# Decay attention with a softplus FFN: product banks as separate tiles, weight pairs of one layer, a read-back of converted weights, and other queues for loads and stores

## The chip, the cores and the metric

The kernel runs on one core of one Trainium2 chip. The metric is the device time of one execution in microseconds (us), the median of several runs. TensorE (PE) does the matmuls, VectorE (DVE) and ScalarE (ACT) the elementwise work, GpSimd (POOL) a few sums; SyncE (SP) issues most DMA transfers from its queue, in the order of the program.

## What is computed

The reference has two stages. First a decay attention over 4 batches, 8 heads, 768 positions of 64 numbers, in blocks of 64 positions with a state carried from block to block:

```python
for b in range(nb):
    intra = einsum('bhic,bhjc->bhij', qb, kb) * Dmask        # lam ** (i - j), i >= j
    intra = einsum('bhij,bhjd->bhid', intra, vb)
    inter = einsum('bhid,bhde->bhie', qb * lam_pow, kv_state)
    out[:, :, sl] = intra + inter
    kv_state = lam_block * kv_state + einsum('bhsd,bhse->bhde', kb * rev_pow, vb)
```

Its output, as 3072 tokens of 512 numbers, goes through an FFN of width 2048:

```python
h = x @ w_in
g = maximum(h, 0) + log1p(exp(-abs(h)))      # softplus
out = g @ w_out
```

All is float32; the weights arrive as float64.

## The kernel before

**Matmuls.** Each FFN operand is split in two rounded parts, high and low, and each product is made of three matmuls (high by high, low by high, high by low), 128x128 weights by 512 columns. Such a matmul takes TensorE 0.227 us.

**Tiling.** The work runs in six chunks of 128 positions by 4 batches, 512 tokens each. A chunk has four attention units, one for each pair of heads (24 units g in all). A unit's inputs come as one tile `att` by two loads of 512 KB (`load_upto`, L86). For each unit: decayed keys (`k_decay`, L287, ACT) and queries (`q_decay`, L294, DVE), scores and state matmuls (`mm_scores`, L309 and L311), the mask (L336, DVE), the state's update (L341, DVE), the output (`mm_out`, L324 and L328), which is then copied out of PSUM (L373, L384 or L391).

**Chunks 0 and 1.** After a prologue written out as a table of steps, a loop runs the steps s = 4 to 31 (`for s in range(LAG, last)`): 16 blocks of 128 of the hidden width, for chunk 0 and then for chunk 1. A step has the first-layer matmuls of block s (`mlp1`, L419, 12 matmuls into a bank `h`), softplus and the split of the block before (`chain_act` L400 and `chain_hi` L404 on ACT, `chain_lo` L408 on DVE), and the second-layer matmuls of the block four steps before (`mlp2`, L436). In chunk 0 every third step holds a unit's scores and two steps later its output; in chunk 1 every second step is an `event`, which has the output of the last unit and the scores of the next.

**Conversion of weights.** In chunk 0 the float64 words are turned into high and low parts, two blocks (a pair) in each step: `w_scale` (L215) and `w_round` (L219) on ACT, `w_shift` (L223), `w_sign` (L227) and `w_add` (L233) on DVE in one step; `w_hi` (L236, ACT) and `w_lo` (L240, DVE) in the next one. `w_order` says which blocks make a pair. Before, a pair is one block of the second layer and one of the first, (f, 1) and (f + 4, 0). All converted weights stay in SBUF through chunk 1. During steps 8 to 23 `store_blocks` (L501 to L504) writes them to DRAM too, in g1 and g2 (first layer) and g3 (second layer). In chunk 1, for each two blocks, POOL forms sums of their quarters (`block_sums`), ACT and DVE split these (`store_sums`, L525 and L526, the tile `parts`), and SP stores them (L528, L529).

**Chunks 2 to 5.** These go in twos (2 with 3, 4 with 5) through a Strassen scheme with seven products where eight would be needed. Each of eight iterations i loads the weights of two blocks from DRAM (`load_w1` L535 and L536, `load_w2` L541) and forms, from weights and token sums prepared before, the products P1, P6, P5, P2, P7, P4, P3 (`product`, L577, six matmuls each). Additions on DVE join them; softplus and splits on ACT and DVE follow. The 24 second-layer matmuls (`rest`, L596) of the iteration before are set between the products. With chunks 2 and 3, each iteration also has an `event`. After the eight iterations, the second layer of the odd chunk runs as a stretch of pure matmuls. `finish` (L605, L607) copies a chunk's four output banks and stores them.

**PSUM.** There are four banks for outputs (`obank`), two single banks in turns (`bank`: `h`, `x`, `y`, `a`) and one tile of two banks (`work`). An iteration's P1 and P2 go to `a`, a single bank. P6, P7 and P4 go to `b_`, P5 and P3 to `c_`; before, both are halves of the one work tile `bc`. The additions that read them are `u2 = b_ + p1` (L737), `u3 = b_ + p1` (L744), `u3 += c_` (L745), `c21 = b_ + p1` (L750) and `u2 += c_` (L754).

**What sets the order.** The program is written in the order in which each engine runs it; nothing is reordered later. An engine waits where a tile that it reads is not written yet, or where a tile that it writes is still being read. For such a wait a tile is one thing, its halves are not told apart. Tiles come from pools of buffers: 21 of 8 KB a partition (`t8`: `att`, weights, outputs), 7 of 4 KB, 5 of 2 KB; a load into a buffer waits until the last reader of what was there is done, and holds up what stands behind it in its queue.

Of the kernel before, what the change touches and what calls it, by code (L numbers as in the profile page):

```python
# [32 lines left out]
def decay_attention_softplus_ffn(  # L33
# [79 lines left out]
    w_order = [(f, 0) for f in range(LAG)]  # L113
    for f in range(NF):
        w_order.append((f, 1))
        if f + LAG < NF:
            w_order.append((f + LAG, 0))
    NW = len(w_order)
# [123 lines left out]
    def w_of(f, which):  # L242
        j, i = divmod(w_order.index((f, which)), 2)
        return w_pairs[j][:, :, i]
# [165 lines left out]
    def mlp1(s, ps_=range(NP)):  # L410
# [4 lines left out]
        for p in ps_:  # L415
            cs = slice(p * 128, (p + 1) * 128)
            x = x_of(c, p)
            for n, (i, j) in enumerate(((0, 0), (1, 0), (0, 1))):
# [3 lines left out]
                )  # L422

    def mlp2(ss):
        c = ss[0] // NF
# [5 lines left out]
        for b in range(B):  # L431
            for s in ss:
                f = s % NF
                g, w = g_tiles[s], w_of(f, 1)
                for n, (i, j) in enumerate(((0, 0), (0, 1), (1, 0))):
                    nc.tensor.matmul(  # L436
                        o_tiles[c][b], lhsT=g[:, i, b * 128 : (b + 1) * 128], rhs=w[:, j],
                        start=f == 0 and n == 0, stop=f == NF - 1 and n == 2,
                    )
# [82 lines left out]
    def store_sums(i):  # L522
# [3 lines left out]
        nc.vector.tensor_sub(out=parts[:, 1], in0=sums, in1=parts[:, 0])  # L526
        parts = parts.bitcast(F32)
        nc.sync.dma_start(out=g1[i][:, :, 2:4], in_=parts[:, :, 0:2])  # L528
# [72 lines left out]
    def finish(c, b):  # L601
        if c not in obs:
            obs[c] = t8([128, B, 512], F32, f"ob{c}")
        copy = nc.vector.tensor_copy if b % 2 else nc.scalar.copy
        copy(out=obs[c][:, b], in_=outs[c, b])  # L605
        queue = nc.scalar if c == NCH - 1 and b % 2 == 0 else nc.sync
        queue.dma_start(out=out[b * S + c * C : b * S + (c + 1) * C, :], in_=obs[c][:, b])  # L607
# [37 lines left out]
    for s in range(LAG, last):  # L645
        if s + 1 in units_at:
            k_decay(units_at[s + 1])
            q_decay(units_at[s + 1])
        chain_act(s - 1)
        chain_hi(s - 1)  # L650
        chain_lo(s - 1)
        old, new = w_group(s - 1), w_group(s)
        if old:
            w_hi(*old)
        if new:
            w_scale(*new)
            w_round(*new)
        if old:
            w_lo(*old)
        if new:  # L660
# [19 lines left out]
        w_load(2 * s + (8 if s < 9 else 6))  # L680
        if s in units_at:
            load_upto(units_at[s] + 2)
        if s == NF - 2:
            load_upto(2 * NP + 2)
        if 8 <= s < 8 + NF:
# [13 lines left out]
        if s == last - 1:  # L699
            x_sums_early(2, 1)  # L700
    x_sums_late(2, 1)
    chain_act(last - 1)
    chain_hi(last - 1)
    chain_lo(last - 1)

    def old_seconds(ss, ends=False):
        return seconds(STD - 1, [(s % NF, g_tiles[s], w_of(s % NF, 1)) for s in ss], ends)

# [5 lines left out]
    for c in range(STD, NCH, 2):  # L714
        more = c + 2 < NCH
        lb = {}
        gs = {}
        for i in range(NF // 2):
            if i + 1 < NF // 2:
                load_w1(i + 1)  # L720
            load_w2(i)
            unit = nxt if more else None
            if unit is not None and unit < NG:
# [7 lines left out]
            p1, u2, u3, c21 = ta[:, 0], ta[:, 1], tb[:, 0], tb[:, 1]  # L731
            a, bc = bank(f"a{c}_{i}"), work(f"bc{c}_{i}")
            b_, c_ = bc[:, 0], bc[:, 1]
            product("P1", i, a)
            nc.scalar.copy(out=p1, in_=a)  # L735
            product("P6", i, b_)
            nc.vector.tensor_add(out=u2, in0=b_, in1=p1)  # L737
            product("P5", i, c_)
            product("P2", i, a, False)
# [17 lines left out]
            if unit is not None and unit <= NG:  # L757
                event(unit)
                load_upto(unit + 2)
                nxt += 1  # L760
# [71 lines left out]
```

## Time and profile before

| | |
|---|---|
| median of 3 runs | 649.57 us (649.55 to 650.25) |
| profiled execution, its own time | 651.41 us |
| its span in the profile | 649.6 us |
| mean granted TensorE clock | 0.991 |
| prologue and chunk 0 | 0 to about 137 us |
| chunk 1 | about 137 to 250 us |
| products of chunk 2 | 250 to 410 us |
| second layer of chunk 3 | 410.5 to 455.6 us |
| products of chunk 4 | about 456 to 593 us |
| second layer of chunk 5 | 592.6 to 645.7 us |

The profile is of one execution; times in it count from the span's start. Its rows name an instruction by engine, line and tiles (written <- read), with buffer numbers left out, and give its start and duration; x12 is a run of twelve alike; in brackets stands how long the engine was idle before and what ended that. A chain of waits follows the last instruction back to what released it. The waits add up who waited for whom. A windows row gives the stretch, its length, each engine's busy time and instructions, the granted TensorE clock (1.00 is full speed), the share of time in which DMA was busy, and GB/s.

### The profile page before, as it was taken

How to read it: one execution, taken by the hardware profiler on the slowest of the kernel's cores; microseconds unless marked ns; L12 is line 12 of the kernel's file. 1: busy time of each engine (PE TensorE's matmuls, PEld its weight loads, DVE VectorE, ACT ScalarE, POOL GpSimd, SP SyncE). 2: the span in 40 equal slices, each digit the busy share in tenths (PEclk: the TensorE clock that was granted, in tenths of full speed). 3: DMA queues.
4: the chain of work that ended last, by engine and by line, in shares of the span. 5: the costliest groups of instructions: out<-in, count | busy, mean ns of one | idle time of the engine just before them, and what ended most of it. 6: DMA issues, size and time to landing. Idle time of an engine off the chain costs nothing.

```text
span 649.6 us, 11970 instructions
## 1 busy us (share of the span) xinstructions
PE 595.5 (92%) x5203; PEld 469.9 (72%) x5203; DVE 307.4 (47%) x452; ACT 251.6 (39%) x408; POOL 51.2 (8%) x59
## 2 busy tenths in 40 slices
PE   8899999599889999798998988999888988889997
PEld 6677888477678877676776766888666777667886
DVE  7689998463456476424424333491232222223410
ACT  4678776441444354332233322550222222223310
POOL 2000000254333500000000000000000000000000
PEclk9999999899999999989999999999999999999999
DMA  8997455657885567597435440395089542300911
GB/s 302 407 406 264 163 186 188 227 179 237 294 268 192 180 216 287 180 399 289 172 132 182 174 164 31 112 423 210 0 346 420 189 153 98 122 1 16 362 75 66
DMA packets 37445, 135.01 MB, mean 208 GB/s; under 512 B 3600, under 2 KB 5648, under 8 KB 31248
## 3 DMA queue, kind: packets, MB, share of 16 engines
q1 hardware_dynamic: 37104, 133.71, 56.5%
q8 instruction: 41, 0.67, 0.4%
q10 hardware_dynamic: 288, 0.52, 0.2%
q14 instruction: 12, 0.10, 0.0%
HBM read 104.86 MB, written 29.36 MB: 207 GB/s over the span
## 4 chain that ended last, share of the span: by engine, by line
PE 63%; DVE 13%; DMA 13%; ACT 4%; SPq 3%; issue 3%; DVEq 0%; ACTq 0%
PE o L596 24%; PE bc L577 19%; DMA att<-in_att 9%; PE a L577 6%; PE o L436 5%; PE h L419 5%; DMA raw<-in_wts 3%; DVE tb L744 2%; DVE tb L745 2%; DVE tb L750 2%; DVE ta L737 2%; PE z L324 1%; DVE parts L526 1%; ACT parts L525 1%; SPq L86 1%
## 5 line engine op out<-in xcount | busy, mean ns | idle before, releaser
L596 PE MATMUL o<-w,g 128*128 128x512 f32 x816 | 192.7, 390 | 0.0
L596 PEld LDWEIGHTS o<-w,g 128*128 128x128 f32 x816 | 152.6, 188 | 32.0
L419 PE MATMUL h<-x,w 128*128 128x512 f32 x384 | 93.4, 394 | 0.0
L436 PE MATMUL o<-w,g 128*128 128x512 f32 x336 | 85.3, 403 | 7.4 <-ACT w L236 6.2
L577 PE MATMUL bc<-xcP,w1b 128*128 128x512 f32 x288 | 77.5, 404 | 14.9 <-DVE tb L750 12.5
L419 PEld LDWEIGHTS h<-x,w 128*128 128x128 f32 x384 | 71.0, 188 | 16.7 <-issue 1.2
L436 PEld LDWEIGHTS o<-w,g 128*128 128x128 f32 x336 | 63.9, 193 | 22.8 <-ACT w L236 7.0
L577 PEld LDWEIGHTS bc<-xcP,w1b 128*128 128x128 f32 x288 | 51.7, 188 | 38.3 <-DVE tb L750 19.4
L577 PE MATMUL bc<-xcP,w1a 128*128 128x512 f32 x192 | 51.3, 403 | 15.4 <-DVE ta L737 15.4
L577 PEld LDWEIGHTS bc<-xcP,w1a 128*128 128x128 f32 x192 | 34.9, 188 | 28.8 <-DVE ta L737 22.2
L577 PE MATMUL a<-xcP,w1a 128*128 128x512 f32 x192 | 50.0, 397 | 0.0
L744 DVE TENSOR_TENSOR tb<-bc,ta 128x512 f32<-128x512 f32 x16 | 11.1, 692 | 73.1 <-PE bc L577 73.1
L577 PEld LDWEIGHTS a<-xcP,w1a 128*128 128x128 f32 x192 | 36.9, 192 | 8.0
L287 ACT ACTIVATE kd<-att,rp 128x256 f32<-128x256 f32 x40 | 18.2, 504 | 61.2 <-DMA att<-in_att 61.2
L737 DVE TENSOR_TENSOR ta<-bc,ta 128x512 f32<-128x512 f32 x16 | 11.1, 692 | 60.0 <-PE bc L577 58.0
L741 ACT ACTIVATE la<-a 128x512 f32<-128x512 f32 x16 | 9.6, 599 | 74.2 <-PE a L577 74.2
L408 DVE TENSOR_TENSOR g<-l,g 128x512 fp32r<-128x512 f32 x32 | 23.2, 724 | 25.0 <-ACT g L404 24.8
L588 DVE TENSOR_TENSOR g<-lb,g 128x512 fp32r<-128x512 f32 x32 | 21.1, 690 | 22.1 <-ACT g L584 22.1
L294 DVE TENSOR_TENSOR qd<-att,lp 128x512 f32<-128x512 f32 x20 | 16.1, 805 | 32.5 <-DMA att<-in_att 32.5
L512 POOL TENSOR_TENSOR full<-w 128x512 f32<-128x512 f32 x16 | 21.4, 1360 | 117.9 <-PE o L436 114.7
L735 ACT COPY ta<-a 128x512 f32<-128x512 f32 x16 | 9.3, 584 | 53.6 <-PE a L577 53.6
L584 ACT CAST g<-lb 128x512 fp32r<-128x512 f32 x32 | 18.9, 620 | 20.3 <-PE o L596 20.3
(96 smaller groups left out, 701.9 us busy)
## 6 DMA issues: line engine op xcount, KB each, us to landing
w<-g SPq DMA_DIRECT2D x32, 1024.0 KB, 9.0
att<-in_att SPq DMA_DIRECT2D x48, 512.0 KB, 6.6
raw<-in_wts SPq DMA_DIRECT2D x32, 512.0 KB, 10.2
w1a<-g SPq DMA_DIRECT2D x16, 1024.0 KB, 8.3
g<-w SPq DMA_DIRECT2D x24, 512.0 KB, 7.4
w1b<-g SPq DMA_DIRECT2D x16, 768.0 KB, 8.9
g<-parts SPq DMA_DIRECT2D x16, 512.0 KB, 4.3
out_dram<-ob SPq DMA_DIRECT2D x22, 256.0 KB, 2.2
```

The lines of the kernel that those rows point to most:

```text
L287: nc.scalar.activation(kd[:, :, t], kt_of(g)[:, :, t], AF.Copy, scale=rp1[:, h : h + 1])
L294: eng.tensor_mul(out=qd[r].rearrange("q b t i -> q b (t i)"), in0=q_of(g)[r].rearrange("q b t i -> q b (t i)"), in1=w)
L408: nc.vector.tensor_sub(out=g[:, 1, :], in0=l_tiles.pop(s), in1=g[:, 0, :])
L419: nc.tensor.matmul(h_tiles[s], lhsT=w[:, i, cs], rhs=x[:, j, :], start=p == 0 and n == 0, stop=p == NP - 1 and n == 2,)
L436: nc.tensor.matmul(o_tiles[c][b], lhsT=g[:, i, b * 128 : (b + 1) * 128], rhs=w[:, j], start=f == 0 and n == 0, stop=f == NF - 1 and n == 2,)
L512: nc.gpsimd.tensor_add(out=full[:, n], in0=w[:, 0], in1=w[:, 1])
L577: nc.tensor.matmul(to, lhsT=w[:, k, n, p * 128 : (p + 1) * 128], rhs=x[:, j, p], start=start and p == 0 and m == 0, stop=p == 1 and m == 2 ...
L584: nc.scalar.copy(out=g[:, 0], in_=l)
L588: nc.vector.tensor_sub(out=g[:, 1], in0=l, in1=g[:, 0])
L596: nc.tensor.matmul(outs[c, b], lhsT=g[:, i, b * 128 : (b + 1) * 128], rhs=w[:, j], start=f == 0 and n == 0, stop=f == NF - 1 and n == 2,)
L737: nc.vector.tensor_add(out=u2, in0=b_, in1=p1)
L744: nc.vector.tensor_add(out=u3, in0=b_, in1=p1)
```

## The change

The eight parts:

1. `w_order`: from block 2 on, a pair is two blocks of one layer, (f, 1) with (f + 1, 1), then (f + 4, 0) with (f + 5, 0). The first-layer block of an even step is so made one step later than before: its `w_hi` and `w_lo` are in the same step as its matmuls. Second-layer blocks are made earlier against their use, or as early.
2. In a step, `w_hi` of the last pair comes ahead of softplus, and `w_lo` ahead of `chain_lo`.
3. In chunk 1 the second layer, from block 2 on, takes its weights from tiles that are read back from g3 (`w_second`, `load_w2` at steps 18, 20 to 30, seven loads of 1024 KB).
4. `store_sums` is cut in two: the split as before, the two stores (`send_sums`) in the next even step.
5. `load_upto` runs a unit further ahead from step 16 on, and in chunk 2 stands at the iteration's start, ahead of the weights' loads, not behind the event.
6. `finish` for all chunks but the last has all four copies on ACT and the stores on ACT's queue (before, copies of odd batches on DVE, stores on SP).
7. The late token sums `x_sums_late(2, 1)` come behind the last softplus and its split.
8. `b_` is the first bank of the work tile, `c_` a single bank from `bank`, asked for after P6: two tiles.

```diff
     w_order = [(f, 0) for f in range(LAG)]
-    for f in range(NF):
-        w_order.append((f, 1))
+    for f in range(2):
+        w_order += [(f, 1), (f + LAG, 0)]
+    for f in range(2, NF, 2):
+        w_order += [(f, 1), (f + 1, 1)]
         if f + LAG < NF:
-            w_order.append((f + LAG, 0))
+            w_order += [(f + LAG, 0), (f + LAG + 1, 0)]
...
+    def w_second(s):
+        f = s % NF
+        return w_of(f, 1) if s < NF or f < 2 else w2_tiles[f // 2][:, f % 2]
...
-                g, w = g_tiles[s], w_of(f, 1)
+                g, w = g_tiles[s], w_second(s)
...
-        parts = parts.bitcast(F32)
+        ready[i] = parts.bitcast(F32)
+
+    ready = {}
+
+    def send_sums(i):
+        parts = ready.pop(i)
         nc.sync.dma_start(out=g1[i][:, :, 2:4], in_=parts[:, :, 0:2])
         nc.sync.dma_start(out=g2[i][:, :, 1:3], in_=parts[:, :, 2:4])
...
-        copy = nc.vector.tensor_copy if b % 2 else nc.scalar.copy
+        end = c == NCH - 1 and b % 2
+        copy = nc.vector.tensor_copy if end else nc.scalar.copy
         copy(out=obs[c][:, b], in_=outs[c, b])
-        queue = nc.scalar if c == NCH - 1 and b % 2 == 0 else nc.sync
+        queue = nc.sync if end else nc.scalar
...
-        chain_act(s - 1)
-        chain_hi(s - 1)
-        chain_lo(s - 1)
         old, new = w_group(s - 1), w_group(s)
         if old:
             w_hi(*old)
+        chain_act(s - 1)
+        chain_hi(s - 1)
+        if old:
+            w_lo(*old)
+        chain_lo(s - 1)
         if new:
             w_scale(*new)
             w_round(*new)
-        if old:
-            w_lo(*old)
...
-        if s in units_at:
+        if s in units_at and s < NF - 2:
             load_upto(units_at[s] + 2)
-        if s == NF - 2:
-            load_upto(2 * NP + 2)
+        if s >= NF - 2 and s % 2 == 0:
+            load_upto(2 * NP + 2 + (s - NF + 2) // 2 + (s >= NF))
+        if s > NF and s % 2 == 0:
+            load_w2((s - NF) // 2)
+        if s > NF + 1 and s % 2 == 0:
+            send_sums((s - NF) // 2 - 1)
...
-    x_sums_late(2, 1)
+    send_sums(NF // 2 - 1)
     chain_act(last - 1)
     chain_hi(last - 1)
     chain_lo(last - 1)
+    x_sums_late(2, 1)
...
+            unit = nxt if more else None
+            if unit is not None:
+                load_upto(unit + 2)
             if i + 1 < NF // 2:
                 load_w1(i + 1)
             load_w2(i)
...
-            a, bc = bank(f"a{c}_{i}"), work(f"bc{c}_{i}")
-            b_, c_ = bc[:, 0], bc[:, 1]
+            a, b_ = bank(f"a{c}_{i}"), work(f"b{c}_{i}")[:, 0]
             product("P1", i, a)
             nc.scalar.copy(out=p1, in_=a)
             product("P6", i, b_)
             nc.vector.tensor_add(out=u2, in0=b_, in1=p1)
+            c_ = bank(f"c{c}_{i}")
             product("P5", i, c_)
...
                 event(unit)
-                load_upto(unit + 2)
```

What stands where, at three places. First TensorE in the fourth iteration of chunk 4; `a` is the single bank, `bc` the work tile, `b` and `c` the tiles in its place, `w1a` and `w1b` the loaded weights. Before:

```order
L577 MATMUL a_3_4832<-xcP_4279,w1a_4730 128x512 x6
L577 MATMUL bc_3_4833<-xcP_4378,w1a_4730 128x512 x6
L577 MATMUL bc_3_4833<-xcP_4355,w1a_4730 128x512 x6
L577 MATMUL a_3_4832<-xcP_4316,w1a_4730 128x512 x6
L577 MATMUL bc_3_4833<-xcP_4381,w1b_4731 128x512 x6
```

And after the change:

```order
L588 MATMUL a_3_4857<-xcP_4301,w1a_4754 128x512 x6
L588 MATMUL b_3_4858<-xcP_4400,w1a_4754 128x512 x6
L588 MATMUL c_3_4873<-xcP_4377,w1a_4754 128x512 x6
L588 MATMUL a_3_4857<-xcP_4338,w1a_4754 128x512 x6
L588 MATMUL b_3_4858<-xcP_4403,w1b_4755 128x512 x6
```

The order of the products is the same; the second and third of them no longer write one tile.

Second ScalarE in steps 7 and 8 of chunk 0; `kd` are decayed keys, `l` softplus and `g` its high part, `c` a pair in conversion, `w` its high part, `raw` its words. Before:

```order
L287 ACTIVATE kd_900<-att_855,rp_128 128x4x64 x2
L400 ACTIVATE l_905<-h_884 128x512
L404 CAST g_907<-l_905 128x512
L236 CAST w_910<-c_865 128x1024
L215 ACTIVATE c_912<-raw_770 128x1024
```

And after the change:

```order
L289 ACTIVATE kd_900<-att_855,rp_128 128x4x64 x2
L238 CAST w_905<-c_866 128x1024
L402 ACTIVATE l_907<-h_884 128x512
L406 CAST g_909<-l_907 128x512
L217 ACTIVATE c_913<-raw_770 128x1024
```

The high part of the last pair has moved from behind the softplus and its split to ahead of them.

Third SP's queue early in chunk 1; `att` is a unit's load, `out_dram` the output of chunk 0, `g` the DRAM copies, `parts` the split sums of two blocks, `w_1` and `w_2` read-backs. Before:

```order
L528 DMA g_0_617<-parts_1661 256x1x512
L529 DMA g_0_625<-parts_1661 256x1x512
L444 DMA out_dram<-ob_1760 128x512 x4
L86 DMA att_1794<-in_att 128x1024 x2
L503 DMA g_5_622<-w_989 256x1x512
L504 DMA g_5_638<-w_1289 128x2x512
L501 DMA g_5_630<-w_1073 256x1x256
L504 DMA g_5_638<-w_1338 128x2x512
L528 DMA g_1_618<-parts_1832 256x1x512
L529 DMA g_1_626<-parts_1832 256x1x512
L86 DMA att_1960<-in_att 128x1024 x2
```

And after the change:

```order
L450 DMA out_dram<-ob_1761 128x512 x4
L86 DMA att_1795<-in_att 128x1024 x2
L552 DMA w_1_1798<-g_1_634 128x2048
L539 DMA g_0_617<-parts_1664 256x1x512
L540 DMA g_0_625<-parts_1664 256x1x512
L509 DMA g_5_622<-w_1068 256x1x512
L510 DMA g_5_638<-w_1284 128x2x512
L507 DMA g_5_630<-w_1068 256x1x256
L510 DMA g_5_638<-w_1284 128x2x512
L86 DMA att_1963<-in_att 128x1024 x2
L552 DMA w_2_1966<-g_2_635 128x2048
```

The sums of a double step now stand behind the next unit's load and a read-back, where before the load stood behind the sums.

More of the change, by code (lines that the diff above doesn't have):

```diff
@@ L704, in decay_attention_softplus_ffn @@
     chain_lo(last - 1)
+    x_sums_late(2, 1)
     def old_seconds(ss, ends=False):
-        return seconds(STD - 1, [(s % NF, g_tiles[s], w_of(s % NF, 1)) for s in ss], ends)
+        return seconds(STD - 1, [(s % NF, g_tiles[s], w_second(s)) for s in ss], ends)
     for b in range(B):
@@ L721, in decay_attention_softplus_ffn @@
             load_w2(i)
-            unit = nxt if more else None
             if unit is not None and unit < NG:
```

## The prediction, made before the changed kernel ran

> **What bounds the kernel now.** I read the page first, then the waits, then the stages one by one. Two lines of the page carry the start: the busy time by engine, and the shares of the chain that ended last.
>
> ```profile
> PE 595.5 (92%) x5203; PEld 469.9 (72%) x5203; DVE 307.4 (47%) x452; ACT 251.6 (39%) x408; POOL 51.2 (8%) x59
> ...
> PE 63%; DVE 13%; DMA 13%; ACT 4%; SPq 3%; issue 3%; DVEq 0%; ACTq 0%
> ```
>
> TensorE is the bound: of the span of 649.6 us it is busy for 595.5, so 54.1 are idle. The change removes no matmul, so a gain comes out of the idle time, out of the pipeline refilling behind it, or out of the clock. Who ends the idle time stands in the waits (who waited for whom, total, times, longest):
>
> ```profile
> PE bc L577 <- DVE ta L737: 15.4, 16, 2.6
> PE bc L577 <- DVE tb L750: 12.5, 16, 0.8
> ...
> SPq L607 <- ACT ob L605: 122.6, 8, 40.9
> SPq L528 <- DVE parts L526: 68.3, 8, 12.0
> ```
>
> The first two are the products of chunks 2 to 5, sixteen iterations in all: 27.9 us of the 54.1. The last two are SP's queue: SP, which issues nearly every load, stands behind stores whose data isn't made yet. That doesn't cost TensorE by itself; the loads queued behind it do, as below.
>
> **Products' banks (part 8 of the list).** One iteration of chunk 4, where no load is late; first the chain, then three of TensorE's rows beside it (start, us, group, idle before).
>
> ```profile
> 473.26 1.36 PE a L577 x6
> 474.62 1.37 PE bc L577 x6
> ...
> 476.08 0.70 DVE ta L737
> ...
> 476.83 1.65 PE bc L577 x6
> ...
> 481.24 0.70 DVE tb L744
> ...
> 481.97 0.70 DVE tb L745
> ...
> 482.71 1.69 PE bc L577 x6
> ...
> 484.42 0.70 DVE tb L750
> ...
> 485.17 1.66 PE bc L577 x6
> 486.82 4.08 PE o L596 x18
> 490.91 1.13 PE a L577 x5
> ```
>
> ```profile
> 476.83 1.65 PE L577 MATMUL bc<-xcP,w1a 128*128 128x512 f32 x6 [0.85 <-DVE ta L737]
> ...
> 479.68 1.52 PE L577 MATMUL bc<-xcP,w1b 128*128 128x512 f32 x6
> 481.04 1.52 PE L596 MATMUL o<-w,g 128*128 128x512 f32 x6
> ```
>
> P5 (476.83) writes the half of `bc` that P6 did not write, and yet it starts only behind VectorE's addition that reads P6's half (476.08): the tile is one. P4 (482.71) waits for the additions of 481.24 and 481.97, P3 (485.17) for that of 484.42. An iteration lasts 490.91 - 473.26 = 17.65 us. Without a wait it is seven products of 1.365 and 24 second-layer matmuls at 4.08/18 = 0.227, together 15.0. The difference of 2.65 is idle time, and the 0.3 by which a product that has waited is longer (1.65 against 1.36).
>
> With `b_` and `c_` apart, P5 needs only the previous iteration's last addition, over long before. What is late next: P7 overwrites `b_` and needs the first addition, which ends at 476.08 + 0.70, while P7 then starts at 474.62 + 3 x 1.365 = 478.7: 1.9 to spare. P4 needs the addition of 481.24 only, which ends 0.70 behind P7's end; six `o` matmuls (1.36) lie between, so 0.4 to 0.5 to spare. P3 needs the second addition, 0.7 behind that, with another product between: 1.1 to spare. So all three waits go and none comes: 16 x 2.65 = **42.4** (bounds: 37.4 if P4's 0.3 stayed in each, 42.4 if nothing does). P6 waits as it did.
>
> **Loads ahead and output stores off SP, in chunk 2 (parts 5 and 6).** The second iteration of chunk 2, in the chain and in TensorE's rows:
>
> ```profile
> 267.06 6.25 DMA att<-in_att
> ```
>
> ```profile
> 275.48 2.09 PE L577 MATMUL bc<-xcP,w1a 128*128 128x512 f32 x6 [2.62 <-DVE ta L737]
> 277.37 2.71 PE L577 MATMUL a<-xcP,w1a 128*128 128x512 f32 x6
> 279.92 1.55 PE L577 MATMUL bc<-xcP,w1b 128*128 128x512 f32 x6
> ```
>
> An `att` load leaves SP only after the output stores of chunk 1; the decayed keys wait for it on ScalarE, behind them the copy of P1, behind that the addition, and P5 stands 2.62 us instead of 0.85. P5 to P7 then takes 4.44 us (275.48 to 279.92), against 2.85 in chunk 4 (476.83 to 479.68), since the clock halved. That is 1.77 + 1.59 = 3.4 beyond the 2.65. In the changed kernel this unit is loaded an iteration earlier, and the stores go out on ScalarE's queue, which is idle for most of the time; each costs ScalarE a copy of some 0.6 us twice more per chunk, under 4 us of second-layer matmuls. I take **3.4** (bounds 0 and 3.4).
>
> [...]
>
> **Read-back and sums sent later, in chunk 1 (parts 3 to 5).** TensorE in chunk 1 (us, busy of each engine, clock, DMA share, GB/s), and the load on which it stands, in the chain:
>
> ```profile
> 139.60:253.00 113.40, 107.26 (x1293) 88.08 (x1291) 60.14 (x91) 48.79 (x85) 36.41 (x40) 1.00 0.66 224
> ```
>
> ```profile
> 168.91 6.94 DMA att<-in_att
> ```
>
> 113.40 - 107.26 = 6.1 us of idle; with the 0.3 of refilling behind each stall, and five stalls (an estimate), 7.5. The stalls come from SP: it waits for `parts` (68.3 us in all), then issues the `att` load of the next unit, which lands when that unit is due. In the changed kernel the two stores of the sums go out two steps later, when they are long made, and the loads run a unit further ahead. Against it stand seven loads more, and their price in DMA time is on the page:
>
> ```profile
> w<-g SPq DMA_DIRECT2D x32, 1024.0 KB, 9.0
> att<-in_att SPq DMA_DIRECT2D x48, 512.0 KB, 6.6
> ```
>
> A read-back is issued four steps (some 26 us) before its first matmul, and takes 9.0. In steps 18 to 23 a double step then moves 1024 KB of `att`, 1024 of read-back, 1024 of sums and 1792 of blocks: 4.98 MB in 13.2 us, 378 GB/s, against 298 now (without the 1.05 MB of the read-back). The page's fullest slices move 407 GB/s, nearly all reads; the stretch of chunk 1 as a whole runs at a share of 0.66. So it fits, with little to spare for three double steps, and then falls to 240. I take **6** of the 7.5 (bounds 0 and 7.5; below nothing is rival D).
>
> [...]
>
> **Weights in pairs of one layer, and the other order in a step (parts 1 and 2).** TensorE's rows give the pace of chunk 0, ScalarE's and VectorE's the durations of one conversion:
>
> ```profile
> 72.60 3.02 PE L419 MATMUL h<-x,w 128*128 128x512 f32 x12
> ...
> 91.56 3.02 PE L419 MATMUL h<-x,w 128*128 128x512 f32 x12
> ```
>
> ```profile
> 69.53 0.62 ACT L404 CAST g<-l 128x512 fp32r<-128x512 f32 x1
> 71.65 1.05 ACT L236 CAST w<-c 128x1024 fp32r<-128x1024 f32 x1 [1.50 <-DVE c L233]
> 72.60 1.14 ACT L215 ACTIVATE c<-raw 128x1024 f32<-128x1024 f32 x1
> ```
>
> ```profile
> 73.87 0.69 DVE L223 TENSOR_SCALAR c<-c 128x1024 uint32<-128x1024 uint32 x1
> 74.59 1.23 DVE L227 SCALAR_TENSOR_TENSOR c<-raw,c 128x1024 uint32<-128x1024 uint32 x1
> 75.96 1.23 DVE L233 CUSTOM_DVE_ANT_0 c<-raw,c 128x2048 uint16<-128x2048 uint16 x1
> ```
>
> TensorE takes 18.96 us for three steps (72.60 to 91.56). Before, a step's ScalarE work does not begin with `w_hi`; after, `w_hi` (which waits for the previous step's addition) is ahead of softplus, and scale stands behind all of it. That closes a ring through both engines: addition 1.23, `w_hi` 0.95, softplus 0.60, its high part 0.62, scale 1.14, shift 0.72, sign 1.37 = 6.6 us a step. In a step with a unit's scores VectorE masks them and advances the state first (some 2.5 us), and its ring of addition, mask, states, `w_lo`, low part, shift and sign is 7.5. Three steps need 2 x 6.6 + 7.5 = 20.7 by this count, more than TensorE's 18.96: conversion becomes the bound of steps 6 to 15, and an even step, whose first-layer weights are now made in the step itself, has TensorE stand for up to 2 us. Over nine steps that makes some 3 x 1.8 = 5 to 8 us late at step 14. But there TensorE stands already now:
>
> ```profile
> 126.81 0.80 PE L436 MATMUL o<-w,g 128*128 128x512 f32 x1 [5.81 <-ACT w L236]
> ```
>
> ```profile
> 126.80:133.10 6.30, 5.82 (x12) 3.76 (x12) 6.10 (x7) 4.74 (x6) 4.86 (x4) 0.50 0.40 82
> ```
>
> It waits 5.81 us for `w_hi`, behind an `att` load on ScalarE, and the clock is then half for 6.3. This hole takes up what comes late from ahead of it: in the new order the late pair is a first-layer pair, the second-layer matmuls (clock and all) no longer stand behind it, and by the same recurrence the next unit's output is due at 134.3 to 135.3 us against 134.55. I take **+1** (bounds: -10 if the hole goes, +6 if the delay and the hole add up).
>
> The move of the late token sums behind the last softplus and the POOL sums cost nothing that I can find: the second-layer matmuls between (12 to 24 of 0.227) cover 0.7 us of ScalarE.
>
> **The sum.** -42.4 - 3.4 - 6 + 1 = -50.8. The profiled execution took 651.41 us (span 649.6), which is 1.84 above the median of 649.57; so 600.6 by its own measure, 598.8 by the median: **599**.
>
> **Rivals.**
> - A, the hole at 121 to 133 us goes: the order of `w_hi` first gets the pair done before the load is waited for. For it: nothing of the hole is matmul work. Against it: the ring of 20.7 against 18.96. Time 599 - 11 = 588.
> - B, the read-backs crowd the `att` loads of chunk 1, and its gain is not had. For it: 378 GB/s wanted. Against it: 407 reached. Time 599 + 6 = 605.
> - C, the change does not do what it says: P4 or one of the others keeps a wait, as `c_` takes a bank of the pair that the unit's scores use as well. Price: from 16 x 0.3 = 5 (P4 alone) up to 16 x 1.1 = 18 (P3 alone). Time 604 to 617. Against it: each of these reads ends 0.4 us or more before the product is due.
> - D, slower: in each of the seven double steps the second-layer matmuls wait for their read-back's whole landing, because it takes turns with stores on the same queue. 7 x 9.0 = 63, less 42.4 + 3.4 - 1: 18 longer, 667. It decides for slower only if more than 6.4 of each 9.0 us are exposed. Against it: each is issued some 26 us ahead.
>
> **How the numbers follow.** The forecast gets 0.60, A 0.12, B 0.16, C 0.10, D 0.02. The range is 588 to 612: it takes in A, B, the lower part of C, and the bounds of chunk 0. Leaving 0.2% (1.3 us, about what a measurement of this kernel can tell from no change) aside, every case but D is faster by much: faster 0.97, same 0.01, slower 0.02.
>
> **What would show it.** Right: no wait of a product on the additions in the waits, an iteration of 15.0 us in chunk 4, second iteration of chunk 2 without its 2.62, the start of chunk 2's products some 6 us closer to the first second-layer pair of chunk 1. Wrong: products that still stand behind VectorE; decayed keys or second-layer matmuls of chunk 1 waiting for a load longer than 1 us each; first-layer matmuls in steps 6 to 14 that wait for `w_hi` or `w_lo` for over 3 us a step (which halves the clock too), and an output of the ninth unit that comes much after 135 or before 130.

## The result, and the profile after

The changed kernel takes 600.16 us (median of 4 runs, 599.66 to 601.33), the kernel before 649.91 us (median of 4, 649.55 to 651.25). The ratio is 0.923, with a 95% interval of 0.921 to 0.925: 49.8 us less, where 50.8 were forecast (599 us, range 588 to 612).

The page of the profile after, its span, busy time, chain by engine, and what moved through DMA:

```profile
span 597.7 us, 12023 instructions
...
PE 578.1 (97%) x5203; PEld 471.9 (79%) x5203; DVE 309.6 (52%) x444; ACT 256.6 (43%) x416; POOL 53.3 (9%) x59
...
GB/s 293 406 407 252 178 153 197 276 268 165 186 389 393 408 416 256 328 312 394 226 135 194 198 207 234 173 296 362 133 212 316 145 196 136 145 268 141 62 1 70
...
PE 81%; DMA 11%; DVE 5%; ACT 1%; issue 1%; SPq 1%; DVEq 0%
```

TensorE's idle time has shrunk from 54.1 to 19.6 us, and its own busy time by 17.4, with the same 5203 matmuls: a matmul that follows a wait is counted longer (1.65 us for six in place of 1.52), and so is one at the slower clock (2.71 for the six from 277.37 on in the kernel before, at a clock of 0.53). Now an iteration of chunk 4 in TensorE's rows:

```profile
426.65 1.52 PE L588 MATMUL b<-xcP,w1a 128*128 128x512 f32 x6
428.01 1.52 PE L588 MATMUL c<-xcP,w1a 128*128 128x512 f32 x6
429.37 1.52 PE L588 MATMUL a<-xcP,w1a 128*128 128x512 f32 x6
430.73 1.52 PE L588 MATMUL b<-xcP,w1b 128*128 128x512 f32 x6
432.09 1.52 PE L607 MATMUL o<-w,g 128*128 128x512 f32 x6
433.45 1.52 PE L588 MATMUL b<-xcP,w1b 128*128 128x512 f32 x6
434.81 1.52 PE L588 MATMUL c<-xcP,w1b 128*128 128x512 f32 x6
436.17 4.24 PE L607 MATMUL o<-w,g 128*128 128x512 f32 x18
440.25 1.52 PE L588 MATMUL a<-xcP,w1a 128*128 128x512 f32 x6
```

No row has a bracket: each group starts 1.36 us behind the one before, and nothing is waited for. From one P1 (425.29) to the next (440.25) it is 14.96 us, where the forecast had 15.0 and the kernel before 17.65. The second iteration of chunk 2, which stood 2.62 us before, has no bracket either; its P5 starts 1.36 us behind its P6:

```profile
263.37 1.52 PE L588 MATMUL b<-xcP,w1a 128*128 128x512 f32 x6
264.73 1.52 PE L588 MATMUL c<-xcP,w1a 128*128 128x512 f32 x6
```

The start of chunk 1, in TensorE's rows, and the stretches around it in windows (us, busy by engine, clock, DMA share, GB/s):

```profile
135.48 0.49 PE L326 MATMUL z<-qd,st 64*64 64x64 f32 x8 [4.51 <-DVE st L343]
```

```profile
136.00:141.00 5.00, 5.00 (x130) 4.56 (x123) 3.84 (x7) 1.91 (x4) 0.07 (x1) 0.78 1.03 392
141.00:240.00 99.00, 99.00 (x1263) 81.91 (x1262) 56.72 (x81) 44.39 (x75) 37.69 (x40) 1.00 0.82 311
```

A hole is left at the end of chunk 0, 4.51 us with the clock down behind it (0.78). After it TensorE is busy without a gap; of chunk 1's 99 us, all 99.

Where the time came from, by stage. The stages begin with what is called the first pair of chunk 1 here (the second-layer matmuls right behind the first `event`, in step 16; they are block 13 of chunk 0, since the second layer runs behind the first), with the first P1 of chunk 2, and with the first P1 of chunk 4; the last one ends with the span.

| stage | before | after | difference | forecast |
|---|---|---|---|---|
| to the first pair of chunk 1 | 136.57 | 138.73 | +2.16 | +1 |
| chunk 1 | 113.50 | 106.04 | -7.46 | -6 |
| chunks 2 and 3 | 205.36 | 180.52 | -24.84 | -21.2 - 3.4 |
| chunks 4 and 5 | 194.17 | 172.41 | -21.76 | -21.2 |
| span | 649.6 | 597.7 | -51.9 | -50.8 |

### The profile page after: what moved, and what is told of

It reads as the page before. It is cut to its first block, busy times and chain, and to the rows that moved or that the text cites. A ratio compares the mean times of both kernels' runs of the same rounds, so it can differ in the third digit from the quotient of the medians.

```text
span 597.7 us, 12023 instructions
## 1 busy us (share of the span) xinstructions
PE 578.1 (97%) x5203; PEld 471.9 (79%) x5203; DVE 309.6 (52%) x444; ACT 256.6 (43%) x416; POOL 53.3 (9%) x59
## 4 chain that ended last, share of the span: by engine, by line
PE 81%; DMA 11%; DVE 5%; ACT 1%; issue 1%; SPq 1%; DVEq 0%
PE o L607 31%; PE b L588 11%; PE h L421 9%; PE o L442 9%; PE a L588 7%; PE c L588 7%; DMA raw<-in_wts 6%; DMA g<-w 2%; PE z L326 2%; DMA att<-in_att 2%; PE x L311 2%; PE z L330 1%; DVE c L229 1%; DVE c L235 1%; DVE st L343 1%
## 5 line engine op out<-in xcount | busy, mean ns | idle before, releaser
L607 PE MATMUL o<-w,g 128*128 128x512 f32 x816 | 192.7, 390 | 0.0
L421 PE MATMUL h<-x,w 128*128 128x512 f32 x384 | 96.0, 400 | 3.1 <-DVE w L242 2.8
L442 PE MATMUL o<-w,g 128*128 128x512 f32 x336 | 82.4, 394 | 1.1 <-DVE w L242 0.8
L588 PE MATMUL b<-xcP,w1b 128*128 128x512 f32 x192 | 48.7, 389 | 0.0
L755 DVE TENSOR_TENSOR ta<-b,ta 128x512 f32<-128x512 f32 x16 | 11.1, 691 | 62.9 <-PE b L588 62.9
L588 PEld LDWEIGHTS b<-xcP,w1b 128*128 128x128 f32 x192 | 36.0, 188 | 7.5
L410 DVE TENSOR_TENSOR g<-l,g 128x512 fp32r<-128x512 f32 x32 | 24.8, 774 | 28.6 <-ACT g L406 28.6
L763 DVE TENSOR_TENSOR tb<-b,ta 128x512 f32<-128x512 f32 x16 | 11.1, 691 | 52.7 <-PE b L588 52.7
L402 ACT ACTIVATE l<-h 128x512 f32<-128x512 f32 x32 | 19.0, 594 | 35.2 <-PE h L421 32.2
L338 DVE TENSOR_TENSOR a<-x,mask 128x512 f32<-128x512 f32 x15 | 10.4, 692 | 41.4 <-PE x L311 21.5
L238 ACT CAST w<-c 128x1024 fp32r<-128x1024 f32 (+1 forms) x19 | 17.4, 913 | 29.2 <-DVE c L235 29.2
L326 PEld LDWEIGHTS z<-qd,st 64*64 64x64 f32 x640 | 17.6, 138 | 11.6 <-issue 11.2
```

Source lines behind the costliest of these rows:

```text
L238: nc.scalar.copy(out=w_at(ks)[:, 0], in_=conv[ks[0]].bitcast(F32))
L326: nc.tensor.matmul(w[half(t), s, cols], lhsT=st[r, b, t], rhs=qd[r, b, t], start=True, stop=False)
L402: nc.scalar.activation(l_tiles[s], h_tiles.pop(s), AF.Softplus)
L410: nc.vector.tensor_sub(out=g[:, 1, :], in0=l_tiles.pop(s), in1=g[:, 0, :])
L421: nc.tensor.matmul(h_tiles[s], lhsT=w[:, i, cs], rhs=x[:, j, :], start=p == 0 and n == 0, stop=p == NP - 1 and n == 2,)
L442: nc.tensor.matmul(o_tiles[c][b], lhsT=g[:, i, b * 128 : (b + 1) * 128], rhs=w[:, j], start=f == 0 and n == 0, stop=f == NF - 1 and n == 2,)
```

## The experiments

The theory to test is the prediction's own: the banks give 42.4; parts 5 and 6 give 3.4 in chunk 2; SP's wait for the split of the sums is what made chunk 1 stand; and chunk 0 loses its pace to the new order in a step, while the hole in front of chunk 1 hides most of that. The rivals stand with the runs. Stage starts of all runs (us in the trace), with the median time and the ratio to the kernel before on the same chip. The kernel before took 649.4 to 652.0 us on the chips used, so small differences are to be read from the ratios and the stage starts, not from the medians of two chips:

| kernel | first pair, chunk 1 | P1, chunk 2 | P1, chunk 4 | median | ratio (95%) |
|---|---|---|---|---|---|
| changed kernel | 138.73 | 244.77 | 425.29 | 600.16 | 0.923 (0.921 to 0.925) |
| part 8 alone | 135.61 | 249.24 | 430.61 | 605.67 | 0.929 (0.926 to 0.932) |
| all but 8 | 140.07 | 246.43 | 448.68 | 644.41 | 0.988 (0.985 to 0.991) |
| all but 4 | 139.23 | 246.13 | 426.63 | 600.94 | 0.922 (0.919 to 0.924) |
| all but 5 in chunk 1 | 139.08 | 249.53 | 430.24 | 604.66 | 0.927 (0.924 to 0.931) |
| all but these two | 139.40 | 254.29 | 434.91 | 608.65 | 0.935 (0.932 to 0.938) |
| all but 6 | 139.89 | 246.10 | 426.57 | 600.57 | 0.924 (0.921 to 0.927) |
| parts 1 and 2 alone | 145.27 | 259.81 | 463.48 | 659.21 | 1.015 (1.012 to 1.017) |
| all but 2 | 134.90 | 241.11 | 421.66 | 595.29 | 0.916 (0.913 to 0.919) |
| all but 3 | 142.77 | 248.77 | 429.25 | 605.39 | 0.930 (0.927 to 0.933) |
| all but 1, 2 and 3 | 137.14 | 243.12 | 423.57 | 598.04 | 0.919 (0.916 to 0.922) |
| mask first in step 15 | 140.21 | 247.78 | 428.32 | 602.27 | 0.927 (0.925 to 0.930) |
| all but 2, mask first | 128.62 | 236.50 | 417.04 | 591.29 | 0.909 (0.906 to 0.911) |

**The banks alone.**

```diff
-            a, bc = bank(f"a{c}_{i}"), work(f"bc{c}_{i}")
-            b_, c_ = bc[:, 0], bc[:, 1]
+            a, b_ = bank(f"a{c}_{i}"), work(f"b{c}_{i}")[:, 0]
...
+            c_ = bank(f"c{c}_{i}")
             product("P5", i, c_)
```

> The kernel before with part 8 alone (b_ and c_ as two tiles). Theory on record: the three waits of each product iteration go and nothing else does, 16 x 2.65 = 42.4 less: 607.5 us; in chunk 4 an iteration takes 15.0 us and no product waits for an addition; chunk 1 (from its first pair of second-layer matmuls to the first product) still takes about 113.5 us, and the second iteration of chunk 2 still stands 2 to 3 us for its late load. Rival: the shorter iterations need the other parts as well (loads and output stores on one queue then come too late for them), and 3 to 10 us of the 42.4 are not had: 610 to 618 us, with products that wait for w1a or w1b.

It took 605.67 us, 46.3 less than the kernel before on the same chip; by the stage starts 45.4 of this lie in chunks 2 to 5. So part 8 alone brings nearly all of the gain. Chunk 1 stood as expected (249.24 - 135.61 = 113.6). Chunks 2 and 3 took 181.37, only 0.85 more than with the whole change, and the rival's late weights did not come. The second iteration of chunk 2, on ScalarE and then on TensorE:

```profile
269.79 0.91 ACT L287 ACTIVATE kd<-att,rp 128x256 f32<-128x256 f32 x2 [3.88 <-DMA att<-in_att]
270.60 0.56 ACT L734 COPY ta<-a 128x512 f32<-128x512 f32 x1
```

```profile
271.22 1.67 PE L577 MATMUL a<-xcP,w1a 128*128 128x512 f32 x6 [0.51 <-ACT ta L734]
```

The `att` load is as late as before, and still stops the copy of P1 for 3.88 us. But the addition behind that copy no longer stops P5; only P2, which overwrites P1's bank, stands for 0.51. So the expected 2 to 3 us of waiting were not there: most of the 3.4 that the prediction gave to parts 5 and 6 goes with the banks.

**All but the banks.** The same edit, undone in the changed kernel.

> The changed kernel with part 8 undone (both banks one tile again), all else kept. Theory on record: the waits come back, 16 x 2.65 = 42.4 more than 600.2: 642.6 us; chunk 0 and chunk 1 as in the changed kernel (first product at about 244.8 us). Rival: part of the gain of chunks 2 to 5 came from the loads and stores of parts 5 and 6, so that less comes back: 630 to 638 us.

It took 644.41, 44.3 more than the changed kernel, 43.1 of it in chunks 2 to 5. Chunks 2 and 3 took 202.25, against 205.36 before: with the banks in one tile, parts 5 and 6, which this run does not separate, do take 3.1 off there, as forecast. TensorE in that second iteration:

```profile
270.47 1.65 PE L588 MATMUL bc<-xcP,w1a 128*128 128x512 f32 x6 [0.85 <-DVE ta L756]
```

0.85 in place of 2.62: the load is on time, the tile's own wait remains. Banks apart, or loads ahead with the output stores off SP: either takes about 3, and together they don't add.

**The sums at once; the loads later; both.** In the first, the two stores stand in the odd step again, right behind the split; in the second, `load_upto` in chunk 1 is as before; the third has both edits.

```diff
-        if s > NF + 1 and s % 2 == 0:
-            send_sums((s - NF) // 2 - 1)
...
             store_sums((s - NF) // 2)
+            send_sums((s - NF) // 2)
```

```diff
-        if s in units_at and s < NF - 2:
+        if s in units_at:
             load_upto(units_at[s] + 2)
-        if s >= NF - 2 and s % 2 == 0:
-            load_upto(2 * NP + 2 + (s - NF + 2) // 2 + (s >= NF))
+        if s == NF - 2:
+            load_upto(2 * NP + 2)
```

> The changed kernel with part 4 undone: the sums' stores are issued right behind their split, in the odd step, so that SP waits for the split again. Theory on record: it is this wait of SP, with a unit's load queued behind it, that made chunk 1 stand; 5 to 7.5 us come back: 605 to 608 us, decayed keys waiting for loads in chunk 1. Rival: the loads that run one unit further ahead are enough by themselves: 600 to 601 us, no TensorE idle time in chunk 1, though SP waits.

> The changed kernel with the part of 5 that lies in chunk 1 undone: a unit's load is issued one unit later, as before; the sums are still sent two steps later. Theory on record (SP's wait for the split is the cause): SP is free when the load's turn comes, and at most 1 us comes back: 600 to 601.5 us. Rival (the run-ahead is what took the stalls away): 605 to 608 us, decayed keys of chunk 1 waiting for loads of 7 to 9 us that are issued one double step before they are due.

Both went against the theory on record. With the sums at once it takes 600.94 us, and chunk 1 takes 106.9, nearly as in the changed kernel (106.04): a load that runs a unit ahead can stand behind the split without harm. With the loads later it takes 604.66, and chunk 1 110.45. TensorE's rows of that kernel have one stall there, and the chain shows what was ahead of it:

```profile
165.22 0.33 PE L311 MATMUL x<-att 64*64 64x64 f32 x2 [0.27 <-ACT l L402]
...
167.31 0.31 PE L313 MATMUL y<-att,kd 64*64 64x64 f32 x1 [1.77 <-ACT l L402]
```

```profile
156.85 1.29 SPq L450
...
158.67 5.08 DMA att<-in_att
```

The stores of chunk 0's output (L450) stand on SP ahead of a unit's load. Part 4 does nothing about them; loading ahead does. That raised the question whether the sums' wait costs anything at all, which the third kernel answers.

> The changed kernel with part 4 and the part of 5 in chunk 1 both undone; read-back kept. Theory now: either of the two takes the unit's load from behind the sums' split (undone alone they cost 0.8 and 4.5 us); without both all of chunk 1's stalls come back, and the seven read-backs are queued with them: 600.2 + 7.5 = 607.7 us or somewhat more, decayed keys waiting in most double steps. Rival: the loads' order against the read-backs and stores is what counts, and it stays near the 604.7 of the later loads alone.

It took 608.65, and chunk 1 takes 114.89, somewhat more than the 113.50 of the kernel before. The stall of the run before is there again, with two more. TensorE's rows:

```profile
166.50 0.33 PE L311 MATMUL x<-att 64*64 64x64 f32 x2 [1.65 <-ACT l L402]
...
210.81 0.27 PE L313 MATMUL y<-att,kd 64*64 64x64 f32 x1 [0.41 <-ACT l L402]
...
239.43 0.27 PE L313 MATMUL y<-att,kd 64*64 64x64 f32 x1 [1.98 <-ACT l L402]
```

The first of these again has the output stores ahead of its load. The load ahead of the second leaves only after a store of sums, as the chain shows:

```profile
195.41 1.24 DVE parts L532
...
197.23 0.62 SPq L540
...
198.80 7.41 DMA att<-in_att
```

So both are causes, SP's wait for the split and SP's wait for the output; loading a unit ahead covers the two, and sending the sums later covers only the first.

**The old output stores.** Part 6 undone in the changed kernel.

```diff
-        end = c == NCH - 1 and b % 2
-        copy = nc.vector.tensor_copy if end else nc.scalar.copy
+        copy = nc.vector.tensor_copy if b % 2 else nc.scalar.copy
         copy(out=obs[c][:, b], in_=outs[c, b])
-        queue = nc.sync if end else nc.scalar
+        queue = nc.scalar if c == NCH - 1 and b % 2 == 0 else nc.sync
```

> The changed kernel with part 6 undone: output copies of odd batches on VectorE, output stores of all chunks but the last on SP. Theory on record: SP stands behind the output stores again, but units are loaded an iteration ahead; 0 to 3.4 us come back in chunk 2's first two iterations: 600.2 to 603.6 us. Rival: with iterations of 15 to 17 us in place of 17.7 to 20, SP's wait makes the weights' loads late as well, and products of chunks 2 and 4 stand for them: 605 us or more.

It took 600.57, and chunks 2 and 3 take 180.47, against 180.52. With the banks apart and the loads ahead, part 6 is worth nothing.

**Pairs of one layer alone.** Parts 1 and 2 put into the kernel before.

```diff
+        old, new = w_group(s - 1), w_group(s)
+        if old:
+            w_hi(*old)
         chain_act(s - 1)
         chain_hi(s - 1)
+        if old:
+            w_lo(*old)
         chain_lo(s - 1)
-        old, new = w_group(s - 1), w_group(s)
-        if old:
-            w_hi(*old)
...
-        if old:
-            w_lo(*old)
```

(and `w_order` as in the change).

> The kernel before with parts 1 and 2 alone (pairs of one layer, the new order in a step). Theory: conversion becomes the bound of steps 6 to 15 (a ring of some 20.7 us for three steps against 18.96 of TensorE), the block of step 15 comes 5 to 8 us later, and the hole at 121 to 133 us takes up all but 1 to 2 us: first pair of second-layer matmuls of chunk 1 at 138 to 139 us, 651 to 652 us in all. Rival: the delay is added behind the hole, or chunk 1's own stalls grow by it: 655 us or more. Other rival: the delay is lost in chunk 1's stalls: 649.9.

It took 659.21: slower than before, by 1.2 to 1.7%. The delay of chunk 0 was added to the hole and not taken up by it: the first pair of chunk 1 comes at 145.27, 8.7 later. The reason stands in SP's row for the load of unit 9, and in VectorE's row ahead of it:

```profile
125.59 0.81 SPq L86 DMA_DIRECT2D att<-in_att  x2
```

```profile
124.34 1.23 DVE L235 CUSTOM_DVE_ANT_0 c<-raw,c 128x2048 uint16<-128x2048 uint16 x1
```

The load goes into the buffer of the last but one pair's words, and leaves when that pair's addition is done (124.34 + 1.23). In the changed kernel the same load leaves at 117.36, at the end of unit 7's output on TensorE, the last reader of that unit's own load:

```profile
117.00 0.30 PE L330 MATMUL z<-a,att 64*64 64x64 f32 x8
```

```profile
117.36 0.80 SPq L86 DMA_DIRECT2D att<-in_att  x2
```

It has another buffer, whose release does not hang on the conversion. The pace of chunk 0 is in TensorE's rows of the changed kernel, and the ring of conversion in ScalarE's:

```profile
83.71 3.02 PE L421 MATMUL h<-x,w 128*128 128x512 f32 x12
...
125.23 3.02 PE L421 MATMUL h<-x,w 128*128 128x512 f32 x12
```

```profile
60.69 1.04 ACT L238 CAST w<-c 128x1024 fp32r<-128x1024 f32 x1 [1.88 <-DVE c L235]
...
67.32 1.05 ACT L238 CAST w<-c 128x1024 fp32r<-128x1024 f32 x1 [2.30 <-DVE c L235]
...
74.81 1.05 ACT L238 CAST w<-c 128x1024 fp32r<-128x1024 f32 x1 [2.40 <-DVE c L235]
...
81.43 1.05 ACT L238 CAST w<-c 128x1024 fp32r<-128x1024 f32 x1 [1.88 <-DVE c L235]
```

The two rows of TensorE are the first-layer matmuls of steps 9 and 15: 41.52 us for six steps, 20.8 for three, where the prediction's ring gave 20.7. The rows of ScalarE are `w_hi` in four steps running, each behind the addition on VectorE: 6.6, 7.5 and 6.6 us apart, as the prediction's count had them.

**Without the read-back; without parts 1 to 3.** In the first, `w_second` returns the kept weights and `load_w2` is left out of chunk 1; in the second `w_order` and the step's order are as before too.

```diff
-        return w_of(f, 1) if s < NF or f < 2 else w2_tiles[f // 2][:, f % 2]
+        return w_of(f, 1)
...
-        if s > NF and s % 2 == 0:
-            load_w2((s - NF) // 2)
```

> The changed kernel with part 3 undone: second-layer weights of chunk 1 are kept from chunk 0, none is read back, 7 MB less is loaded. Theory: the read-back's use is to free buffers, so that units can be loaded ahead; without it the loads wait for buffers that are released late in chunk 1 and the stalls come back: 604 to 608 us. Rival: there are buffers enough, and the read-back buys nothing: 599.5 to 600.5 us, chunk 1 without idle time.

> The changed kernel with parts 1, 2 and 3 undone: pairs of mixed layers, the order of a step and the kept weights as before; sums' stores, loads, output stores, token sums and banks as changed. Theory (pairs of one layer serve to free buffers by the read-back): chunk 0 as before (first pair of second-layer matmuls of chunk 1 at 135 to 137 us), but units cannot be loaded ahead in chunk 1 and 4 to 7.5 us of stalls come back: 602 to 606 us. Rival: loads ahead do without it, and the whole is 596 to 598 us, better than the changed kernel.

The first took 605.39, as the theory had it, but not for the theory's reason: chunk 1 takes 106.0 and has no idle time behind its start. The loss lies ahead of it, in the same load of unit 9:

```profile
123.89 0.80 SPq L86 DMA_DIRECT2D att<-in_att  x2
```

```profile
122.63 1.23 DVE L235 CUSTOM_DVE_ANT_0 c<-raw,c 128x2048 uint16<-128x2048 uint16 x1
```

Without the read-back the load has the buffer of the words again and waits for the addition; the first pair of chunk 1 comes 4.0 later. The second took 598.04, as its rival said: with the old pairs that addition is early, the load leaves at 116.57, chunk 1 takes 106.0, and the whole is about 2 us below the changed kernel. The two intervals just touch (0.916 to 0.922 against 0.921 to 0.925), so that it is faster is likely, not shown. Parts 1, 2 and 3 together bring nothing that these runs show.

**The old order in a step.** Part 2 alone undone in the changed kernel; pairs of one layer and the read-back stay.

> The changed kernel with part 2 undone: pairs of one layer, but softplus and its split ahead of the pair's high and low parts, as before. Theory (it is the ring through w_hi, softplus, split and scale that slows chunk 0): the ring loses softplus and split, 1.2 us a step, but the first-layer matmuls of an even step now wait for high and low part that stand behind the softplus of the step before, 1 to 2 us in each of five even steps; chunk 0 up to step 15 then takes 2 us less to 4 us more, and the whole 598 to 604 us. [...]

It took 595.29, below the range that the theory gave, and 4.9 below the changed kernel. TensorE's waits for weights in its even steps:

```profile
73.94 1.43 PE L421 MATMUL h<-x,w 128*128 128x512 f32 x5 [0.58 <-DVE w L242]
...
87.77 2.57 PE L421 MATMUL h<-x,w 128*128 128x512 f32 x10 [1.34 <-DVE w L242]
```

They are 0.58 and 1.34; in the changed kernel such waits are 2.05 and 0.76, and one of 1.96 for split tokens stands ahead of them. Six steps, from the first-layer matmuls of step 9 (80.47) to those of step 15 (120.47), take 40.0 us against 41.5, and step 9 itself comes 3.2 earlier. So the old order is worth more than weights which are ready earlier in the step. `w_hi` waits 1.2 us or less for an addition in steps 6 to 14 (1.9 to 2.4 in the rows above), which fits a ring without softplus and split in it. The hole in front of chunk 1 stays, 3.72 us.

**The mask first.** In step 15 the second-layer matmuls, the scores of unit 8, the mask and the state are written ahead of the last pair's shift, sign and addition (and no longer behind them); first in the changed kernel, then in the one with the old order.

```diff
+        if s == NF - 1:
+            mlp2([s - LAG])
+            scores_of(scores_at[s])
+            keep_values(2 * NP)
         if new:
             w_shift(*new)
...
-        if s - 1 not in both_at:
+        if s - 1 not in both_at and s != NF - 1:
             mlp2([s - LAG])
-        if s in scores_at:
+        if s in scores_at and s != NF - 1:
```

> The changed kernel with one move of its own: in step 15 the second-layer matmuls and the scores of the ninth unit are written ahead of the conversion of the last pair, so that VectorE masks the scores and advances the state before it shifts, signs and adds, not behind it. Theory: what is left of the hole at the start of chunk 1 (TensorE idle 4.5 us for the state, and the clock halved behind it, 1.2 us) is the conversion of 5 us ahead of the mask; it goes, and nothing waits for the last pair, which is used some 15 us later: 594.5 us, the first pair of second-layer matmuls of chunk 1 at 133 us. Rival: the unit's output waits for the decayed keys' load instead, or the last pair now comes too late: 599 to 601 us.

It took 602.27: nothing gained, by a wait that neither side had named. ScalarE and TensorE:

```profile
136.71 1.04 ACT L238 CAST w<-c 128x1024 fp32r<-128x1024 f32 x1 [6.34 <-DVE c L235]
137.66 0.59 ACT L402 ACTIVATE l<-h 128x512 f32<-128x512 f32 x1
```

```profile
138.30 0.36 PE L313 MATMUL y<-att,kd 64*64 64x64 f32 x1 [5.61 <-ACT l L402]
```

Unit 9's state matmuls write the bank from which the softplus of step 15 reads, and that softplus now stands behind the last pair's `w_hi`, which waits 6.34 us for the delayed addition. It is part 2 that put it there, so the same move was tried without it.

> The changed kernel with part 2 undone (softplus and split ahead of the pair's high part, as in the run at 595.3 us) and, in step 15, scores, mask and state ahead of the conversion of the last pair. Theory: in the run with the mask first alone, the next unit's state matmuls waited 5.6 us for a bank whose softplus stood behind the last pair's high part; with softplus ahead of it that wait is gone, and the 3.7 us for the state with the slower clock behind them (7.3 us at 0.77) go: 595.3 - 3.7 - 1.3 = 590 us. Rival: the last pair's high part, now later, holds up the copies behind it on ScalarE, and the wait moves on once more: 594 to 596 us.

It took 591.29: the ratio to the kernel before is 0.909 (0.906 to 0.911), the best of all here. The first pair of chunk 1 comes at 128.62, and one wait is left, 1.46 us for the next unit's mask:

```profile
133.10 5.73 PE L421 MATMUL h<-x,w 128*128 128x512 f32 x24 [1.46 <-DVE a L338]
```

The mean granted clock is 1.00 over the whole span.

## Why the prediction was right, and where its reasons were not

**Banks.** Right, mechanism and size: 2.65 forecast for an iteration, 17.65 - 14.96 = 2.69 measured, and no product waits for an addition. Rival C is out, and so is D; A did not come either, for the hole ahead of chunk 1 stayed (4.51 us).

**Chunk 2.** The size was right, 24.84 for chunks 2 and 3 against 24.6. The step that failed is the one that gave 3.4 of it to loads ahead and output stores on ScalarE's queue, on top of what the banks give. The banks alone brought all but 0.85, and part 6, undone with the banks apart, nothing. The late load hurt through the addition for which P5 stood, and that link was cut by the banks. Behind the 1.59 that the forecast put down to the clock stand these windows of the kernel before, P5 up to the start of P2, and P2 up to that of P7; the granted clock in them was 0.77 and 0.50:

```profile
275.48:277.37 1.89, 1.89 (x7) 1.51 (x7) 0.00 (x0) 0.00 (x0) 0.00 (x0) 0.77 0.95 307
277.37:279.92 2.55, 2.55 (x7) 1.97 (x6) 0.00 (x0) 0.00 (x0) 0.00 (x0) 0.50 1.02 396
```

**Chunk 1.** -7.46 against -6, all of the 7.5 that the prediction had as its upper bound. Rival B (read-backs that crowd the loads) did not come: the page's slices 12 to 15 moved 389 to 416 GB/s, above the 378 asked for. The step that failed is the cause given, that the stalls come from SP's wait for the sums. That is one cause, and the output stores of chunk 0 are another; part 5 takes away both, and part 4 adds little to it at most (chunk 1 is 0.86 us longer without it).

**Chunk 0.** +2.16 against +1. The ring was sized well (20.7 forecast, 20.8 measured), step 15's first-layer matmuls came 7.2 late (117.99 before, 125.23 after, 5 to 8 forecast), and the hole took up most of that. But the reason given for the last was wrong, and so the size came out near by luck. The reason was that the pair which comes late is now a first-layer one; by `w_order` it is (12, 1) with (13, 1), of the second layer, before and after, and the same pairs without parts 3 to 8 came 8.7 late. The hole takes up the delay where the load of unit 9 gets another buffer, and that hangs on the read-back: without it alone the first pair came 4.0 later than in the changed kernel. The other 2.5 between that run and the one with parts 1 and 2 alone were not traced. So the bound of +6, delay and hole together, was the right answer for parts 1 and 2 by themselves, and a little short. The prediction also put the POOL sums at nothing. In the changed kernel they run beside the work of VectorE which the state at the end of the hole waits for: from 126.63 on, the low part of the tokens, shift, sign and addition took 1.79, 1.23, 1.64 and 1.53 us, where a step earlier they took 0.69, 0.70, 1.23 and 1.23. The sum of the differences is 2.3 us, which is an estimate of what the sums add to the 4.51 that TensorE waits; no run leaves them out.

**The sum.** The misses of chunk 1 (1.5 more than forecast) and of chunk 0 (1.2 less) nearly cancel, so that the total is closer than its terms.

**What was not asked.** Whether each part is needed. Part 2 costs 4.9 us, parts 4 and 6 bring less than 1, and parts 1 to 3 together bring nothing that these runs can tell. Part 7, and the half of part 5 that lies in chunk 2, were not undone by themselves.

## What to carry to other kernels

Two halves of one tile, written and read by turns, made a matmul wait for a reader of the other half (P5 for 0.85 us in chunk 4 of the kernel before); look for waits in which the writer and its releaser touch different parts of a tile. Here they went when the second half became a tile of its own, in a bank that was free in time, at no cost that a run shows. Where engines feed one another in a step, add up the ring of what each one's order puts between (here 6.6 us a step, and by the same count 5.4 without softplus and split): an operation set early "to be ready" can lengthen the ring by what it is set ahead of, if it has to wait (part 2 cost 4.9 us). And a part that looks like the cure of a stall is tested by undoing it alone and with its neighbour: two cures of one stall did not add here, and a load's lateness can hang on which buffer it is given.

## What the runs showed of the hardware that I had not expected

VectorE's work was slower while GpSimd formed its sums. VectorE, and then GpSimd, in the kernel with the mask first:

```profile
132.31 2.17 DVE L229 SCALAR_TENSOR_TENSOR c<-raw,c 128x1024 uint32<-128x1024 uint32 x1
134.61 2.06 DVE L235 CUSTOM_DVE_ANT_0 c<-raw,c 128x2048 uint16<-128x2048 uint16 x1
```

```profile
131.80 3.79 POOL L518 TENSOR_TENSOR full<-w 128x512 f32<-128x512 f32 x2
```

The same two take 1.23 us each in chunk 0, where GpSimd rests (120.32 and 121.68 in the changed kernel), so the rows show 0.8 to 0.9 us more for an instruction beside GpSimd; why is not shown. Transfers did not slow such work here: in the changed kernel the low part of the tokens (L410) took 1.79 us at 126.63, beside GpSimd and with little moved (DMA share 0.21 from 126.6 to 128.4), and 0.68 at 137.07, where GpSimd rested and DMA was busy all the time (share 1.05 from 137.0 to 137.8). Nor was every instruction slower: the mask (L338), which reads one of its inputs from PSUM, took 0.68 us at 132.83 in the changed kernel, beside GpSimd (131.90 to 133.49), and 0.69 at 138.85, where GpSimd rested.

And much the same stall had the clock at half in one kernel and not in another. TensorE stands 1.10 and 1.77 us for unit 11 in the kernel before (163.16 and 165.25), and 0.96 and 1.77 with the banks alone (162.05 and 164.14). The windows behind that, first of the kernel before, then with the banks alone:

```profile
164.30:170.90 6.60, 5.65 (x82) 4.79 (x83) 4.38 (x8) 2.52 (x5) 1.39 (x3) 1.00 0.71 237
```

```profile
163.20:169.80 6.60, 5.66 (x71) 4.77 (x72) 4.46 (x8) 2.51 (x5) 0.00 (x0) 0.50 0.80 259
```

The granted clock is 1.00 in the first and 0.50 in the second; what decides is not shown here. Behind the longer waits of the kernel before and the changed one it was 0.50: after 5.81 us from 126.80 to 133.10 and after 2.62 us from 277.37 to 279.92 in the kernel before, after 4.51 us from 135.50 to 137.70 in the changed one.
